# A gated linear attention with a feed-forward layer: pairs of chunks in an order made by a list scheduler

## The chip, the cores and the metric

The kernel runs on one core of one Trainium2 chip. The core has five engines that run side by side, each in its own order: TensorE (PE, matrix products), VectorE (DVE), ScalarE (ACT), GpSimd (POOL) and SyncE (SP, which issues most of the transfers). The metric is the device time of one execution in microseconds (us), the median of several runs.

## The reference

Per batch (4), head (8) and step (768) a complex gate of width 48 decays a state of 48 x 48; q reads it. Then each of the 3072 tokens of 384 goes through a normalised two-layer product.

```python
mag = np.sqrt(a_re * a_re + a_im * a_im)
scale = np.minimum(mag, 0.999) / (mag + 1e-06)
...
for t in range(S):
    new_re = ar * S_re - ai * S_im
    new_im = ar * S_im + ai * S_re
    S_re, S_im = (new_re + kv, new_im)      # kv = k[t] (x) v[t]
    y[:, :, t] = np.einsum('bhd,bhde->bhe', q[:, :, t], S_re)
...
xn = (x - mu) / np.sqrt(var + 1e-06) * g_ln
out = x + np.maximum(xn @ w_ch1, 0.0) @ w_ch2
```

## The kernel before

The steps are cut into 24 chunks of 128 (six per batch), number n. Four chunks make a group, number qi; a group has two blocks of 256 steps. In a block's tiles of the gate, partition p holds steps 2p and 2p+1.

The log stage works on a whole group (the first group on one block at a time). ScalarE takes the logarithm `w` of a_re and 1/a_re (`g_log`), VectorE the ratio `r` of imaginary to real part and its square `r2` (`g_ratio`), ScalarE log(1 + r2) (`g_log1p`), VectorE the log of the magnitude `l` (`g_decay`), ScalarE the angle `th` = arctan r (`g_angle`). ScalarE has one table of functions for logarithm and exponential and one for arctan and sine, and loads the one that is needed (`table`).

Sums over the steps are matrix products with triangular matrices. `s_decay` sums `l` for a block with `u_f`, in matmuls of 64 rows that lie in the two halves of the array by turns, and ScalarE makes the growth `en` and the decay `e` of it. `s_phase` sums the angle for one chunk, twice: the first for the sine, the second a quarter turn on for the cosine. Each sum has two matmuls of 64 rows with `u_th` (L406) and one with `pick` (L409), which adds the running phase that VectorE carries from chunk to chunk in `car` (L413). The low 16 bits of the sum are the fraction of a turn, and ScalarE takes the sine of both (`trig`). `s_total` and `s_total2` make the decay of a whole chunk (`et`, `dec`).

GpSimd scales k by `en` and q by `e` (`s_scale`, L421, tiles `ke` and `qe`); VectorE multiplies each by cosine and sine (`s_stack`, `ks` and `qs`). Per chunk, TensorE transposes both (`transp`), forms the scores (`amat`), the next state (`state`, tile `G`) and the output x (`yout`), and transposes x (`xtr`). VectorE and ScalarE carry the results from the sum memory. The feed-forward layer (MoE in the code) works on a group, 512 tokens: `mm1` with 512 columns, ScalarE's Relu, then `mm2` per chunk, VectorE's last step `ot`, and the store. The weights are scaled by `moe_g_ln` and centred once, by column means from TensorE (`w_scale`, `w_centre`).

SP issues the loads of the gate, of k and q, and the stores. GpSimd's queue issues four loads of v and the two weight loads, each of which also casts to 16 bits.

The order comes from `PLACES`, a table of numbers in units of chunks: each step is put at its chunk's number plus its place, and `plan.run()` emits the steps sorted by it. GpSimd keeps the order as written; for the other engines the framework may still order what is ready. The first group has an order written out by hand.

Of the kernel before, what the change touches and what calls it, by code (L numbers as in the profile page):

```python
# [24 lines left out]
class Plan:  # L25


    def __init__(self):
        self.items = []

    def add(self, at, thunk):
        self.items.append((at, len(self.items), thunk))

    def spread(self, lo, hi, thunks):
        for i, t in enumerate(thunks):
            self.add(lo + (hi - lo) * (i + 0.5) / len(thunks), t)

    def run(self):
        for _, _, t in sorted(self.items, key=lambda x: x[:2]):
            t()  # L40


class Ledger:


    def __init__(self):
        self.keys = set()

    def step(self, made, needs):
        for key in needs:  # L50
# [5 lines left out]
     'load_qk_step': 1.29,
     'table_log': -1.2,
     'log': -1.36,  # L60
     'ratio': -0.91,
     'log1p': -0.58,
     'decay': -0.03,
     'sum': 0.72,
     'sum_step': 0.02,
     'total': 0.75,
     'total2': 6.05,
     'table_trig': 1.15,
     'angle': 1.51,
     'phase': 2.17,  # L70
     'phase_step': 0.59,
     'ke': 1.89,
     'ke_step': 0.17,
     'qe': 1.75,
     'qe_step': 0.6,
     'stack_k': 3.93,
     'stack_q': 3.62,
     'stack_step': 1.02},
 2: {'load_a': -7.2,
     'load_qk': -0.53,  # L80
     'load_qk_step': 1.29,
     'table_log': -1.2,
     'log': -0.78,
     'ratio': -0.59,
     'log1p': -0.14,
     'decay': -0.03,
     'sum': 0.75,
     'sum_step': 0.02,
     'total': 0.73,
     'total2': 5.58,  # L90
     'table_trig': 1.04,
     'angle': -0.31,
     'phase': 1.21,
     'phase_step': 0.21,
     'ke': 1.89,
     'ke_step': 0.16,
     'qe': 1.16,
     'qe_step': 0.77,
     'stack_k': 3.93,
     'stack_q': 3.62,  # L100
     'stack_step': 1.02},
 3: {'load_a': -7.56,
     'load_qk': -0.59,
     'load_qk_step': 1.29,
     'table_log': -1.2,
     'log': -0.86,
     'ratio': -0.75,
     'log1p': -0.48,
     'decay': -0.03,
     'sum': 0.42,  # L110
     'sum_step': 0.14,
     'total': 0.7,
     'total2': 5.71,
     'table_trig': 1.31,
     'angle': 0.73,
     'phase': 1.31,
     'phase_step': 0.1,
     'ke': 1.02,
     'ke_step': 0.16,
     'qe': 2.24,  # L120
     'qe_step': 0.02,
     'stack_k': 3.88,
     'stack_q': 3.65,
     'stack_step': 0.07},
 'first': {'ks': -1.65, 'qs': -1.23, 'amat': 0.63, 'state': 0.9, 'yout': 1.0, 'xtr': 1.46},
 'chunk': {'ks': 0.42, 'qs': 0.18, 'amat': 1.14, 'state': 2.6, 'yout': 2.06, 'xtr': 2.49},
 'moe': {'mm1': 6.4, 'mm1_len': 1.89, 'mm2': 8.05, 'mm2_len': 1.88},
 'rstd': 7.32,
 'end_log': -2.06,
 'load_v': -5.9,  # L130
 'w_lo': 2.93,
 'w_hi': 6.07,
 'second': {'ks': -0.32, 'qs': -0.41, 'amat': 0.99, 'state': 1.69, 'yout': 2.49, 'xtr': 3.13},
 'start': -2.01,
 'start_step': 0.09}
# [3 lines left out]
def kernel(  # L139
# [29 lines left out]
    consts = ctx.enter_context(tc.tile_pool(name="consts", bufs=1))
    wts = ctx.enter_context(tc.tile_pool(name="wts", bufs=1))  # L170
    ld = ctx.enter_context(tc.tile_pool(name="ld", bufs=2))
    pr = ctx.enter_context(tc.tile_pool(name="pr", bufs=1))
    stk = ctx.enter_context(tc.tile_pool(name="stk", bufs=2))
    att = ctx.enter_context(tc.tile_pool(name="att", bufs=2))
    msb = ctx.enter_context(tc.tile_pool(name="msb", bufs=2))
    pa = ctx.enter_context(tc.tile_pool(name="pa", bufs=4, space=PSUM))
    pb = ctx.enter_context(tc.tile_pool(name="pb", bufs=2, space=PSUM))

    ctx.enter_context(tc.manual_schedule(engines={mybir.EngineType.Pool}))

    def bank(shape, dtype, name):
        return pa.tile(shape, dtype, tag="a", name=name)

    def two_banks(name):
        return pb.tile([C, 2, 512], FP32, tag="b", name=name)


    Q = [dict() for _ in range(NQ)]
    X = [dict() for _ in range(N)]
    V = {}  # L190
    step = Ledger().step

    def load_a(qi, k_):

        b, blk = divmod(qi * QB + k_, NCH // R)
        step(("a", qi, k_), [])
        for name, ap in (("are", a_re), ("aim", a_im)):
            if name not in Q[qi]:
                Q[qi][name] = ld.tile([C, QB, H, R * D], FP32, tag=name, name=name)
            nc.sync.dma_start(  # L200
                out=Q[qi][name][:, k_],
                in_=ap[b].rearrange("h (k p j) d -> p k h (j d)", p=C, j=R)[:, blk])

    def load_qk(qi, m):
        step(("qk", qi, m), [])
        b, c = divmod(qi * QC + m, NCH)
        for name, ap in (("k", k), ("q", q)):
            X[qi * QC + m][name] = ld.tile([C, H, D], FP32, tag=name, name=name, bufs=6)
            nc.sync.dma_start(out=X[qi * QC + m][name],
                              in_=ap[b].rearrange("h (c p) d -> p c h d", p=C)[:, c])  # L210

    def load_v(b):
        step(("v", b), [])
        V[b] = ld.tile([C, H, NCH, D], BF16, tag="v", name="v", bufs=3)
        nc.gpsimd.dma_start(out=V[b], in_=v[b].rearrange("h (c p) d -> p h c d", p=C))

    load_a(0, 0)
    load_a(0, 1)


    ident = consts.tile([C, C], BF16)
    make_identity(nc, ident)

    u_f = consts.tile([C, R, C], FP16)
    u_hi = consts.tile([C, R, C], FP16)
    for t, base in ((u_f, 0), (u_hi, C)):
        nc.gpsimd.memset(t, 1.0)
        nc.gpsimd.affine_select(out=t, in_=t, pattern=[[-1, R], [1, C]], compare_op=ALU.is_ge,
                                fill=0.0, base=base, channel_multiplier=-R)
    nc.gpsimd.affine_select(out=u_hi, in_=u_hi, pattern=[[0, R], [0, C]], compare_op=ALU.is_ge,  # L230
                            fill=0.0, base=-HALF, channel_multiplier=1)
    nc.vector.tensor_tensor(out=u_f, in0=u_f, in1=u_hi, op=ALU.add)
    u_th = consts.tile([C, R, C], FP16)
    nc.vector.tensor_scalar(out=u_th, in0=u_f, scalar1=INV2PI, scalar2=None, op0=ALU.mult)


# [419 lines left out]
```

## Time and profile before

| | us |
|---|---|
| runs | 268.26, 269.4, 336.7 |
| median | 269.4 |
| profiled execution, span from first to last instruction | 266.8 |
| profiled execution's own time | not listed apart; the two runs that lie together are 1.5 and 2.6 above its span |
| TensorE busy | 214.6 |
| ScalarE, VectorE, GpSimd busy | 172.0, 168.4, 65.6 |

Busy times are of the span of one execution. Engines overlap, so they don't add up to it; an engine is the limit only in a stretch in which it has no idle time, and for that one looks at windows of the span.

### The profile page before, as it was taken

To read this page: it belongs to the slowest core of one execution; us is meant where nothing else is said; L and a number is where in the kernel's file an instruction comes from. 1 tells how busy PE (TensorE), PEld (TensorE's weight loads), DVE (VectorE), ACT (ScalarE), POOL (GpSimd) and SP (SyncE) were. 2 spreads that over 40 slices of the span, in tenths; PEclk is the share of its full clock that TensorE was granted. 3 is DMA by queue.
4 is the path that set the end of the run, shared out by engine and by line. 5 is a ranking of instruction groups with operands and counts; after the bars stand their busy time and mean duration, and the time that the engine had idled before them with its cause. 6 is when DMAs were issued, how large, how long until landed. Compare 5 with 4: busy or idle time off the path is not lost.

```text
span 266.8 us, 4741 instructions
## 1 busy us (share of the span) xinstructions
PE 214.6 (80%) x1937; PEld 126.4 (47%) x1953; DVE 168.4 (63%) x280; ACT 172.0 (64%) x199; POOL 65.6 (25%) x90
## 2 busy tenths in 40 slices
PE   0136733248834999999999999999999999999994
PEld 0001313036421556564576555655557677656452
DVE  1434237767877889976699557986588466645011
ACT  4353571482999769996499785998858723751530
POOL 8390008452401940039100090000900000000000
PEclk9999999999985899999799999999999999999999
DMA  7999925999999995727990052000100011001102
GB/s 204 239 272 193 167 45 144 246 189 158 137 183 266 203 140 88 194 74 160 165 90 0 33 117 62 32 0 32 59 0 32 2 59 63 0 2 60 61 29 88
DMA packets 105350, 28.62 MB, mean 107 GB/s; under 512 B 100336, under 2 KB 104944, under 8 KB 105328
## 3 DMA queue, kind: packets, MB, share of 16 engines
q1 hardware_dynamic: 78736, 23.60, 40.6%
q0 software_dynamic: 26592, 4.72, 21.6%
q8 instruction: 15, 0.25, 0.4%
q14 instruction: 7, 0.06, 0.1%
HBM read 28.31 MB, written 4.72 MB: 124 GB/s over the span
## 4 chain that ended last, share of the span: by engine, by line
PE 58%; ACT 17%; DMA 10%; DVE 8%; POOL 3%; issue 2%; SPq 2%; POOLq 0%
PE o L534 17%; PE hps L524 11%; DMA k<-in_k_dram 10%; PE tps L406 7%; PE tp L440 5%; PE tps L409 4%; PE at L452 3%; DVE r L332 3%; ACT r L309 2%; ACT h L527 2%; ACT are L309 2%; ACT w L309 2%; PE lps L368 2%; PE gm L474 2%; ACT L305 2%
## 5 line engine op out<-in xcount | busy, mean ns | idle before, releaser
L534 PE MATMUL o<-w2b,h 128*128 128x384 bf16 x288 | 52.3, 333 | 0.0
L524 PE MATMUL hps<-xT,w1b 128*128 128x512 bf16 x202 | 50.3, 379 | 0.9 <-ACT h L527 0.2
L527 ACT ACTIVATE h<-hps 128x1024 bf16<-128x1024 f32 x36 | 36.5, 1021 | 11.4 <-PE hps L524 11.3
L309 ACT ACTIVATE trig<-tps 128x768 bf16<-128x768 int16 x24 | 19.5, 811 | 27.2 <-DVE car L413 25.6
L534 PEld LDWEIGHTS <-h 128*128 128x128 bf16 x288 | 27.6, 100 | 18.7 <-issue 3.5
L537 DVE SCALAR_TENSOR_TENSOR ot<-o,rstd,x 128x384 f32<-128x384 f32 x24 | 14.8, 617 | 31.5 <-PE o L534 31.5
L454 DVE TENSOR_TENSOR atm<-at,mask 128x1024 bf16<-128x1024 f32 x24 | 29.1, 1213 | 7.1 <-PE at L452 6.9
L387 POOL COPY et<-et 4x384 bf16<-4x384 bf16 x6 | 4.7, 788 | 113.7 <-ACT et L309 113.7
L406 PE MATMUL tps<-th,u_th 64*128 64x384 f16 x96 | 26.4, 358 | 7.6 <-ACT th L309 7.6
L524 PEld LDWEIGHTS <-w1b 128*128 128x128 bf16 x216 | 19.6, 98 | 18.9 <-issue 0.5
L443 ACT COPY qsT<-tp 96x1024 bf16<-96x1024 bf16 x24 | 24.1, 1005 | 4.1 <-PE tp L440 4.1
L368 PE MATMUL lps<-l,u_f 64*128 64x384 f16 x48 | 7.7, 420 | 20.8 <-DVE l L348 20.8
L421 POOL TENSOR_TENSOR ke<-k,en 128x384 bf16<-128x384 f32 x24 | 21.3, 906 | 11.2 <-DMA k<-in_k_dram 7.1
L421 POOL TENSOR_TENSOR qe<-q,e 128x384 bf16<-128x384 f32 x24 | 22.0, 933 | 1.6 <-ACT e L309 1.2
L413 DVE TENSOR_SCALAR car<-tps 32x384 f16<-32x384 int16 x20 | 11.3, 563 | 16.6 <-PE tps L409 16.3
L496 ACT CAST x<-y 128x384 bf16<-128x384 f32 x24 | 11.3, 472 | 16.1 <-PE y L493 16.0
L440 PE MATMUL tp<-ident,qs 128*96 128x128 bf16 x192 | 16.7, 232 | 4.1 <-DVE G L478 4.1
L305 ACT ACT_TABLE_LOAD x14 | 18.0, 1283 | 1.0 <-PEq L642 0.8
L332 DVE TENSOR_TENSOR r<-aim,are 128x1536 f16<-128x1536 f32 (+1 forms) x7 | 10.9, 1562 | 11.9 <-ACT are L309 11.9
L440 PE MATMUL tp<-ident,ks 128*96 128x128 bf16 x192 | 17.2, 233 | 1.3 <-DVE ks L428 1.3
L443 DVE COPY ksT<-tp 96x1024 bf16<-96x1024 bf16 x24 | 16.3, 678 | 2.8 <-PE tp L440 2.6
L409 PE MATMUL tps<-car,pick 128*128 128x384 f16 (+1 forms) x48 | 17.5, 365 | 0.2 <-DVE car L413 0.2
(72 smaller groups left out, 362.8 us busy)
## 6 DMA issues: line engine op xcount, KB each, us to landing
are<-in_a_re_dram SPq DMA_DIRECT2D x12, 384.0 KB, 4.7
aim<-in_a_im_dram SPq DMA_DIRECT2D x12, 384.0 KB, 4.9
k<-in_k_dram SPq DMA_DIRECT2D x24, 192.0 KB, 4.3
q<-in_q_dram SPq DMA_DIRECT2D x24, 192.0 KB, 4.1
out_dram<-ot SPq DMA_DIRECT2D x24, 192.0 KB, 1.8
v<-in_v_dram POOLq DMA_DIRECT2D x4, 576.0 KB, 15.3
w1b<-in_moe_w_ch_dram POOLq DMA_DIRECT2D x1, 1152.0 KB, 9.7
w2b<-in_moe_w_ch_dram POOLq DMA_DIRECT2D x1, 1152.0 KB, 17.7
```

Source lines behind the costliest of these rows:

```text
L305: chain(nc.scalar.preload_act_table_set({"log": "natural_log_exp_and_others", "trig": "trig_and_small"}[name]))
L309: chain(nc.scalar.activation(**kw))
L332: nc.vector.tensor_tensor(out=cut(r, bs), in0=cut(Q[qi]["aim"], bs), in1=cut(Q[qi]["are"], bs), op=ALU.mult)
L406: nc.tensor.matmul(heads(ps[:, s]), lhsT=u_th[ts(i, HALF), j], rhs=steps(Q[qi]["th"], k_, i, j), start=(j == 0), stop=False)
L409: nc.tensor.matmul(ps[:, s, 0:DM], lhsT=pick[rows, s], rhs=cars[n % 2][rows], start=False, stop=True)
L421: eng.tensor_tensor(out=t[:, m], in0=X[qi * QC + m][which].rearrange("p h d -> p (h d)"), in1=Q[qi]["en" if which == "k" else "e"][:, m], ...
L440: nc.tensor.transpose(ps[:, h], Q[qi][which][:, m, h].rearrange("p a d -> p (a d)"), ident)
L443: (nc.scalar.copy if which == "qs" else nc.vector.tensor_copy)(out=t, in_=ps)
L454: nc.vector.tensor_tensor(out=x["atm"], in0=ps, in1=mask.unsqueeze(1).to_broadcast([C, H, C]), op=ALU.mult)
L524: nc.tensor.matmul(ps[:, ji], lhsT=w1b[:, dc, ts(jp * 2 + ji, C)], rhs=Q[qi]["xT"][:, dc].rearrange("p c t -> p (c t)"), start=(dc == 0), ...
L527: nc.scalar.activation(out=h[jp], in_=ps, func=AF.Relu)
L534: nc.tensor.matmul(ps, lhsT=Q[qi]["h"][j // 2][:, j % 2, ts(m, C)], rhs=w2b[:, j], start=(j == 0), stop=(j == NJ - 1))
```

## The change

The kernel is written anew around pairs of chunks (12 pairs, three per batch), with these parts:

- **Order.** Every step is an `Op` in a `Graph`: its engine (or two to choose from), a cost in us, what it needs, which buffers of which ring it uses (`RINGS`) and which banks of the sum memory. `order` places the steps one after another on five engines by their earliest start, and among those that could start soon takes the one with the smallest key (`KEYS` plus the pair's number). All five engines then keep that order.
- **Log stage** per pair, in units of one, one and then two pairs. The square may run on GpSimd or VectorE.
- **Sums.** For a pair, partition p holds steps 2p and 2p+1, and both kinds of sums run over all 128 rows. The phase is summed once per chunk; the carry is made once per pair.
- **Cosine.** ScalarE takes the sine of the angle and of its half (`sh`); the cosine is 1 - 2 sh^2, on GpSimd or VectorE (`f_cos`).
- **Choices of engine.** Scalings of k and q on GpSimd or VectorE; copies of the transposes on VectorE or ScalarE.
- **MoE** on a pair, 256 tokens: matmuls of 256 columns.
- **Weights.** Scaling and centring are one matrix product of the weights with `gc`, 27 matmuls; the two loads stand behind the constants on GpSimd.
- **v** is loaded in 32 bits by SP and cast by GpSimd. `rstd` is a power on GpSimd in place of a logarithm and an exponential on ScalarE.

```diff
-PLACES = {1: {'load_a': -7.56,
-     'load_qk': -0.53,
...
+KEYS = {"ld_a": -10.982, "ld_qk": -2.438, "ld_v": -1.699, "vcast": 4.3, "t_log": -4.145, "ln":
...
+    def order(self, keys):
...
+                    if len(op.alts) > 1:
+                        other = [x for x in op.alts if x != e][0]
+                        if free[other] + op.alts[other][0] < t + op.alts[e][0] - 0.01:
+                            continue
+                    ests.append((t, op))
...
+                t0 = min(x[0] for x in ests) + SLACK[e]
+                t, op = min((x for x in ests if x[0] <= t0), key=lambda x: (x[1].key, x[0]))
...
+    UNITS = [[0], [1], [2, 3], [4, 5], [6, 7], [8, 9], [10, 11]]
...
+    for i in range(2):
+        g.add(("wl", i), "POOL", 1.4, "wl", i, lambda i=i: wl(i), tail=6.7)
...
+            def wp(jb=jb, ec=ec, o=o):
+                for dc in range(ND):
+                    nc.tensor.matmul(bank(o), lhsT=gc[:, dc, ts(ec, C)],
+                                     rhs=w1r[:, dc, ts(jb, 512)], start=(dc == 0),
+                                     stop=(dc == ND - 1))
...
+        add(("v", P), "POOL", .82, lambda: nc.gpsimd.tensor_scalar(
+            out=T("v", P), in0=T("vf", P), scalar1=1.0, scalar2=0.0, op0=ALU.mult, op1=ALU.add),
+            needs=[("vf", P, 0), ("vf", P, 1)], uses=[("vf", P), ("v", P)], key="vcast")
...
+        def f_dec():
+            ps = bank2(("dec", P))
+            for c in range(R):
+                for j in range(R):
+                    nc.tensor.matmul(heads(ps[:, c, 0:DM]), lhsT=u_e[:, c, j], rhs=step(T("l", P), j),
+                                     start=(j == 0), stop=(j == R - 1))
...
+        def f_ph():
+            ps = bank2(("ph", P))
+            rows = slice(0, 96) if first else slice(0, C)
+            for c in range(R):
+                nc.tensor.matmul(ps[:, c, 0:DM], lhsT=pick[rows], rhs=T("car", P)[rows],
+                                 start=True, stop=False)
+                for j in range(R):
+                    nc.tensor.matmul(heads(ps[:, c, 0:DM]), lhsT=u_th[:, c, j], rhs=step(T("th", P), j),
+                                     start=False, stop=(j == R - 1))
...
+        def f_cos():
+            eng = engine(("cos", P))
+            eng.tensor_tensor(out=T("sh", P), in0=T("sh", P), in1=T("sh", P), op=ALU.mult)
+            eng.tensor_scalar(out=T("trig", P)[:, 0], in0=T("sh", P), scalar1=-2.0, scalar2=1.0,
+                              op0=ALU.mult, op1=ALU.add)
...
+                def f_mm1(gi, part, o):
...
+                            nc.tensor.matmul(ps[:, jj], lhsT=w1b[:, dc, ts(gi * JG + jj, C)],
+                                             rhs=T("xT", P)[:, dc].rearrange("p c t -> p (c t)"),
+                                             start=(dc == 0), stop=(dc == ND - 1))
```

On GpSimd, before, from the scalings of the first group to the weight loads (`ke`, `qe` are scaled k and q, the number behind a name is that of its buffer):

```order
L421 TENSOR_TENSOR qe_222<-q_155,e_191 128x384
L215 DMA v_243<-in_v_dram 128x48x48
L387 COPY et_310<-et_310 4x8x48
L421 TENSOR_TENSOR ke_219<-k_157,en_189 128x384
L421 TENSOR_TENSOR ke_219<-k_161,en_189 128x384
L421 TENSOR_TENSOR qe_222<-q_159,e_191 128x384
L421 TENSOR_TENSOR qe_222<-q_163,e_191 128x384
L273 DMA w1b_146<-in_moe_w_ch1_dram 128x3x1536
L274 DMA w2b_147<-in_moe_w_ch2_dram 128x12x384
```

And now, from the last constants on (`v0<-vf0` is the cast of v for pair 0, `r21<-r1` the square for pair 1):

```order
L326 DMA w1r_178<-in_moe_w_ch1_dram 128x3x1536
L304 MEMSET sel_172 128x8
L307 MEMSET sel_172 64x1 x4
L308 MEMSET half_n_174 128x2
L328 DMA w2b_180<-in_moe_w_ch2_dram 128x12x384
L311 MEMSET cmat_175 128x1152
L313 AFFINE_SELECT cmat_175<-cmat_175 128x384 x3
L399 TENSOR_TENSOR qe0_110<-q0_70,e0_99 128x384
L390 TENSOR_SCALAR v0_78<-vf0_76 128x768
L399 TENSOR_TENSOR r21_88<-r1_85 128x768
L399 TENSOR_TENSOR ke1_109<-k1_74,en1_102 128x384
```

The weight loads stood behind the scalings of the first group and now stand ahead of the first of them; a cast of v and the square of pair 1 have come in, in this order.

On VectorE, before, in the middle of the program (`r` ratio, `r2` square, `l` log of the magnitude, `atm` masked scores, `ksT` copy of a transpose):

```order
L428 TENSOR_TENSOR ks_1643<-ke_1260,trig_1332 128x16x48
L332 TENSOR_TENSOR r_1576<-aim_383,are_381 128x1536
L454 TENSOR_TENSOR atm_1545<-at_1546,mask_131 128x1024
L498 BN_STATS stats_1539<-x_1537 128x6
L334 TENSOR_TENSOR r2_1577<-r_1576 128x1536
L499 BN_AGGR mv_1443<-stats_1539 128x2
L443 COPY ksT_1600<-tp_1591 96x1024
```

And now, at the ratios of pairs 6 and 7 (L399 is the helper of all products of two tiles, L360 that of the copies, L629 the last step `ot`):

```order
L399 TENSOR_TENSOR ks1_113<-ke0_108,trig1_104 128x16x48 x2
L399 TENSOR_TENSOR qs1_116<-qe0_110,trig1_104 128x16x48 x2
L629 SCALAR_TENSOR_TENSOR ot1_163<-banks_63,rstd2_154,x4_137 128x384
L360 COPY ksT0_118<-banks_63 96x1024
L360 COPY ksT1_119<-banks_63 96x1024
L399 TENSOR_TENSOR r0_84<-aim0_67,are0_64 128x768
L360 COPY qsT0_122<-banks_63 96x1024
L360 COPY qsT1_123<-banks_63 96x1024
L399 TENSOR_TENSOR ks2_114<-ke1_109,trig2_105 128x16x48
L399 TENSOR_TENSOR atm2_128<-banks_63,mask_171 128x1024
```

The square has left this stretch for GpSimd, the ratios are half as long, and copies of `qsT` stand beside those of `ksT`.

## Rows read from the trace of the kernel before

**Rows 1.** The page: busy us (share, instructions); DMA in tenths by 40 slices.

```profile
PE 214.6 (80%) x1937; PEld 126.4 (47%) x1953; DVE 168.4 (63%) x280; ACT 172.0 (64%) x199; POOL 65.6 (25%) x90
...
DMA  7999925999999995727990052000100011001102
```

**Rows 2.** Two windows: length, busy us of PE, PEld, DVE, ACT, POOL, clock, DMA, GB/s.

```profile
0.00:100.00 100.00, 53.44 (x415) 27.91 (x419) 59.78 (x88) 60.32 (x65) 41.01 (x62) 0.95 1.19 186
100.00:267.00 167.00, 161.17 (x1523) 98.44 (x1534) 108.62 (x193) 111.66 (x134) 24.62 (x28) 0.99 0.29 60
```

**Rows 3.** The chain that ended last, 40 to 75 us: start, us, what.

```profile
46.72 15.72 DMA k<-in_k_dram
...
62.50 9.83 DMA k<-in_k_dram
```

**Rows 4.** Timeline of SP's queue: start, us, what.

```profile
4.22 1.15 SPq L209 DMA_DIRECT2D k<-in_k_dram  x1
...
12.31 0.70 SPq L200 DMA_DIRECT2D are<-in_a_re_dram  x1
...
47.91 4.85 SPq L209 DMA_DIRECT2D q<-in_q_dram  x1
...
62.50 3.53 SPq L209 DMA_DIRECT2D k<-in_k_dram  x1
```

**Rows 5.** The page's DMA issues: size of each, us from issue to landing.

```profile
w2b<-in_moe_w_ch_dram POOLq DMA_DIRECT2D x1, 1152.0 KB, 17.7
```

**Rows 6.** Timeline of TensorE, phase sums.

```profile
121.99 0.50 PE L406 MATMUL tps<-th,u_th 64*128 64x384 f16 x2
...
122.69 0.49 PE L406 MATMUL tps<-th,u_th 64*128 64x384 f16 x2
```

**Rows 7.** The chain that ended last, TensorE at its full rate: start, us, what.

```profile
113.94 0.43 PE lps L368 x4
...
116.01 0.74 PE tot L381 x4
...
119.66 0.45 PE tp L440 x8
...
208.15 2.59 PE hps L524 x12
...
255.15 7.81 PE o L534 x48
```

**Rows 8.** Timeline of the first 40 us.

```profile
8.88 0.93 ACT L309 ACTIVATE r<-r,one_b 128x768 f16<-128x768 f16 x1 [2.93 <-POOL eps_b L264]
...
11.25 0.82 PE L368 MATMUL lps<-l,u_f 64*128 64x384 f16 x4 [11.25 <-DVE l L348]
...
17.44 0.80 PE L406 MATMUL tps<-th,u_th 64*128 64x384 f16 x2 [5.36 <-ACT th L309]
...
23.80 1.03 DVE L428 TENSOR_TENSOR ks<-ke,trig 128x768 bf16<-128x768 bf16 x2 [0.95 <-ACT trig L309]
```

**Rows 9.** Groups by line: count, busy us, mean ns, idle before.

```profile
L443 DVE COPY ksT<-tp 96x1024 bf16<-96x1024 bf16 x24 | 16.3, 678 | 2.8 <-PE tp L440 2.6
...
L421 POOL TENSOR_TENSOR qe<-q,e 128x384 bf16<-128x384 f32 x24 | 22.0, 933 | 1.6 <-ACT e L309 1.2 <-DMA q<-in_q_dram 0.4
...
L413 DVE TENSOR_SCALAR car<-tps 32x384 f16<-32x384 int16 x20 | 11.3, 563 | 16.6 <-PE tps L409 16.3 <-PE gm L474 0.2
```

**Rows 10.** Timeline, GpSimd and VectorE side by side.

```profile
42.46 1.77 POOL L421 TENSOR_TENSOR ke<-k,en 128x384 bf16<-128x384 f32 x2
...
43.48 3.31 DVE L334 TENSOR_TENSOR r<-r 128x1536 f16<-128x1536 f16 x1
...
44.20 1.77 POOL L421 TENSOR_TENSOR qe<-q,e 128x384 bf16<-128x384 f32 x2
...
108.35 0.95 DVE L334 TENSOR_TENSOR r<-r 128x1536 f16<-128x1536 f16 x1
```

**Rows 11.** A window of the first stage, columns as in Rows 2.

```profile
80.00:85.00 5.00, 1.75 (x8) 0.48 (x8) 4.13 (x7) 4.83 (x6) 0.00 (x0) 0.50 1.06 270
```

More of the change, by code (lines that the diff above doesn't have):

```diff
@@ L22 @@
 PSUM = bass.MemoryType.PSUM
[L25 to L52, printed above, removed]
@@ L56 @@
-PLACES = {1: {'load_a': -7.56,
-     'load_qk': -0.53,
[L58 to L135, printed above, removed]
@@ L155 @@
     NCH = S // C
-    N = B * NCH
     R = 2
-    QC = 4
-    QB = QC // R
-    NQ = N // QC
+    PB = NCH // R
+    NP = B * PB
     DM = H * D
@@ L166 @@
     HALF = C // R
+    JG = 4
+    NG = NJ // JG
     INV2PI = 1.0 / (2.0 * PI)
[L169 to L234, printed above, removed]
-    pick = consts.tile([C, 2, C], FP16)
-    nc.gpsimd.memset(pick, 0.0)
-    for s in range(2):
-        for row in (HALF + s, C - 1):
-            nc.gpsimd.affine_select(out=pick[:, s], in_=pick[:, s], pattern=[[0, C]],
+    UNITS = [[0], [1], [2, 3], [4, 5], [6, 7], [8, 9], [10, 11]]
@@ L242, with c_ue2, c_pick @@
+    def c_ue2():
+        nc.gpsimd.affine_select(out=u_e[:, 1], in_=u_e[:, 1], pattern=[[0, R], [0, C]],
+                                compare_op=ALU.is_ge, fill=0.0, base=-HALF, channel_multiplier=1)
+    def c_pick():
+        nc.gpsimd.memset(pick, 0.0)
+        for row in (HALF, C - 1):
+            nc.gpsimd.affine_select(out=pick, in_=pick, pattern=[[0, C]],
                                     compare_op=ALU.not_equal, fill=1.0, base=-row,
                                     channel_multiplier=1)
-    cars = []
@@ L556 @@
-    seq += [lambda m=m, w=w: s_scale(0, w, m) for w in "kq" for m in range(R)]
-    seq += [lambda w=w, a=a: s_stack(0, w, a, pair(0)) for w in "kq" for a in range(2)]
-    for i, t in enumerate(seq):
-        add(-30 + 0.1 * i, t)
-    seq = [lambda: load_v(0), lambda: g_angle(0, one(1)), lambda: s_phase(0, 2),
-            lambda: s_phase(0, 3), lambda: table("log"), lambda: g_log1p(0, one(1)),
-            lambda: g_decay(0, one(1)), lambda: s_decay(0, 1), lambda: s_total(0),
-            lambda: s_total2(0)]
@@ L598 @@
-    for g in range(NQ):
-        add(QC * g + P["rstd"], lambda g=g: rstd(g))
-    for i in range(2):
-        add(QC * (NQ - 1 + i) + P["end_log"], lambda: table("log"))
-    for b in range(1, B):
-        add(b * NCH + P["load_v"], lambda b=b: load_v(b))
-    for n in range(N):
-        o = P["first"] if n < R else P["second"] if n < QC else P["chunk"]
-        add(n + o["ks"], lambda n=n: transp(n, "ks"))
-        add(n + o["qs"], lambda n=n: transp(n, "qs"))
-        add(n + o["amat"], lambda n=n: amat(n))
-        add(n + o["state"], lambda n=n: state(n))
-        add(n + o["yout"], lambda n=n: yout(n))
-        add(n + o["xtr"], lambda n=n: xtr(n))
@@ L623, with c_ident, c_mask, c_sel @@
-    load_a(1, 0)
-    load_a(1, 1)
-    nc.sync.dma_start(out=gln, in_=moe_g_ln.rearrange("(dc p) -> p dc", p=C))
-    for m in range(QC):
-        add(P["start"] + 0.1 * m, lambda m=m: load_qk(1, m))
-    plan.run()
+        for t in tiles["car"]:
+            nc.gpsimd.memset(t, WINDOW)
+    def c_ident():
+        make_identity(nc, ident)
+    def c_mask():
+        make_upper_triangular(nc, mask, val=1.0, diag=True)
+    def c_sel():
+        nc.gpsimd.memset(sel, 0.0)
+        for k_ in range(R):
+            for i in range(R):
+                nc.gpsimd.memset(sel[ts(i, HALF), k_, ds(k_ * R + i, 1)], 1.0)
+        nc.gpsimd.memset(half_n, -0.5)
@@ L631 @@
+    for op in g.order(KEYS):
+        op.emit()
 _INS = ['q', 'k', 'v', 'a_re', 'a_im', 'moe_g_ln', 'moe_w_ch1', 'moe_w_ch2']
```

773 lines of the change are left out of this document (471 added, 302 removed), and 8 rows, old and new, of tables (KEYS, RINGS).

## The prediction

> **What bounds the kernel now.** I read the engines' busy times first. TensorE is busy 214.6 us of a span of 266.8, VectorE 168.4, ScalarE 172.0, GpSimd 65.6, and the DMA row is at 7 to 9 tenths for most of the first third, then nearly empty [rows 1]. Then two windows: from 0 to 100 us TensorE is busy 53.44 us, from 100 us to the end 161.17 of 167 [rows 2]. So there are two stages with two limits. In the second TensorE is full and only its own work counts. In the first it is half idle, and the chain that ended last says for what: it waits 15.72 and 9.83 us in a row for loads of k [rows 3]. The queue shows why. At the start SP passes eight loads of k and q in the 8.1 us between 4.22 and 12.31, about 1.0 us each; between 47.91 and 62.50 it passes three, 4.9 us each [rows 4]. That is while the two weight loads of GpSimd's queue run: the second lands 17.7 us after its issue [rows 5].
>
> **The change, part by part.** TensorE first, all at the rate of the second stage.
>
> Phase sums. Before, each of 24 chunks has two groups of two 64-row sums and one `pick`; one group takes 0.70 us from start to start (121.99 to 122.69) [rows 6]: 48 x 0.70 = 33.6 us. After, each of 12 pairs has two groups of three 128-row sums. A 128-row sum of the same strided 16-bit kind takes 0.74/4 = 0.185 (`tot`), a dense one 7.81/48 = 0.163 (`o`) [rows 7]. So a group costs 0.49 to 0.70; I take 0.56, from the nearest row, `tot`: 24 x 0.56 = 13.4. Gain 20.2 (16.8 to 21.8).
>
> Decay sums. Before, four 64-row sums take 0.43 together, since two halves of the array work side by side [rows 7]: 12 x 0.43 = 5.2. After, four 128-row sums follow one another: 12 x 0.74 = 8.9. Cost 3.7. The Trainium skill (TensorEngine Tiling, When to Use Tiling) says that a contraction of 64 rows is to be packed two to the array, which speaks against this part of the change. The trace agrees for the decay sums, 0.43 against 0.74; by that rule they would stay as they were and TensorE would have 3.7 us less to do.
>
> MoE. The first product goes from 512 to 256 tokens: 216 matmuls at 2.59/12 = 0.216 become 432. Eight matmuls of 128 columns, each with its own weights, take 0.45, 0.056 each [rows 7]; 256 columns lie between that and 0.163 for 384, at 0.109. 432 x 0.109 = 47.1 against 46.7: nothing. The second product is unchanged, 288 x 0.163 = 46.9.
>
> Weights. Nine column means become 27 products of 512 columns: +18 x 0.216 = 3.9. The total decays stay at 24 x 0.185 = 4.4; their spread to 96 rows goes from 48 to 56 small matmuls, +0.4.
>
> The rest per chunk (two transposes, scores, state, output, each eight heads or a little more) I price at 0.45 a piece: about 67 us with the transposes of x and the totals, the same before and after. TensorE in all after the change: 13.4 + 8.9 + 47.1 + 46.9 + 5.8 + 67 = 189 us; 12 less than before.
>
> ScalarE. Two evaluations per chunk as before (sine of the angle and of its half in place of sine and cosine), seven table loads and eleven copies fewer: below 172, and not the bound.
>
> VectorE. Twelve carries of 0.563 go (-6.8); eleven of the transposed copies of 0.678 come from ScalarE (+7.5) [rows 9]; 23 of the 48 scalings of k and q come from GpSimd, at about 0.55, an estimate below the 0.678 of a larger copy (+12.7). The other edits (squares to GpSimd, a smaller weight correction, two cosines, logs in halves) I put at -8, give or take 4. So 168.4 becomes some 174.
>
> GpSimd. It keeps 25 scalings of 0.93 (23 us) and takes ten squares, ten cosines of two steps and twelve casts of v, each on 768 columns. By the 384-column scaling that is 0.93 to 1.9 each; with 1.8 for two-input ones and 1.35 for the others, 18 + 31 + 16. About 88 us beside the constants, never full, but busy some 0.45 of the dense stage.
>
> Loads. v moves from four casting loads of GpSimd's queue to 24 plain ones behind SP: eight loads per pair, 8 us, against 189/12 = 15.8 us of TensorE for a pair. This hides, once the weights are through. But the weights now are issued behind the constants, at about 6 and 8 us instead of 46, beside the first inputs. For 17.7 us SP would pass four loads instead of seventeen: k and q of the first pair, and v of the first pair lands at about 27.5 instead of 15. What is queued behind it: on GpSimd the cast of v stands ahead of the square for pair 1, as the order shows, so pair 1's logs wait with it.
>
> **The first stage after.** In the kernel before, ScalarE's log of the first block starts at 8.88, after 2.93 of waiting for a constant, the sums start at 11.25, the phase sums at 17.44, and the products with sine and cosine at 23.80 [rows 8]. For pair 0 the steps stay: the constant comes first now, which takes off what it held up, a cosine is added, two of the four phase groups fall away; its products end near 24. Then v is last. Six loads of the two a's are out by 7 us, the next four (k, q) pass by 25, the two of v by 27.5. The cast ends at 28.9, the square at 30.7, and pair 1 repeats the steps of [rows 8]: log to sums 2.4, sums to phase sums 6.2, less two ScalarE operations like the 0.93 at 8.88 that stood between, plus some 2.7 for a total, two casts of x and the phase sums themselves: 40 us. On TensorE the weight products and all of MoE stand behind those phase sums, so the dense stage begins at about 40. Without the wait for v it would be 35, the square then standing behind pair 0's products. By then about 10 us of the 189 are done.
>
> **The dense stage.** 179 us remain for TensorE. VectorE has about 174 - 17 = 157 us in it. They are ordered by one list, each in its own order, so what one loses the other waits for. The loss that I see in the trace: VectorE's square at 43.48 took 3.31 us where its like takes 0.95; it stood still while GpSimd ran four scalings from 42.46 on and finished 0.8 us after them [rows 10]. So VectorE's operations on two SBUF inputs and GpSimd's exclude each other. Some 60 runs of such operations on VectorE (products, ratios, logs, scalings) meet GpSimd busy with a chance of 0.45; the wait is 0.55 for the rest of one operation and 2.4 for a row of four. That is 15 us at 0.55, 65 at 2.4, and none if the order keeps them apart. VectorE has 179 - 157 = 22 to spare, so I let half of the 15, 8 us, reach TensorE.
>
> **The sum.** 40 + 179 + 8, and 3.8 from the last `o` (255.15 + 7.81) to the end of the span, as now: 231. The profiled execution's span is 266.8, the median of the runs 269.4, so 2.6 lies around it: **233 us**, 0.865 of the median. A measurement here tells about 2% from no change.
>
> **Rivals.** *TensorE alone.* The order keeps the others out of its way, as in the second stage now, where it idles 6 of 167 us: 233 - 8 = 225, and 220 with the dense stage from 35. For: that stage now. Against: VectorE has less to spare.
>
> *The shared port sets the pace.* The mean wait is 1.3, half of the long one: 60 x 0.45 x 1.3 = 35, VectorE needs 157 + 35 = 192, and with the 8 us of mutual waiting 40 + 192 + 8 + 3.8 + 2.6 = 246; up to 260. For: [rows 10], and GpSimd's work doubled. Against: at 0.45 busy, rows of four are rare. The Trainium skill (SBUF — State Buffer, SBUF: two separate sides) calls this port pair an exclusive lock that one instruction holds to its end; the trace agrees, with 3.31 us for 0.95.
>
> *TensorE falls to the lower clock, and the kernel is slower.* Between 80 and 85 us, with TensorE busy 1.75 of 5, the granted clock is 0.50, which is 1.2 GHz [rows 11]; in the second stage it is 0.99. If waits for VectorE thin TensorE out, every us of its work takes two. From 40 + 179 x (1 + f) + 6.4 = 275 on it would be slower: f = 0.28, 50 us of dense work at the lower clock. Against: TensorE would have to be mostly idle over a quarter of the stage.
>
> **Chances.** The forecast (225 to 240) 0.42, TensorE alone (218 to 225) 0.20, the port (240 to 264) 0.25, the lower clock 0.06; 0.07 is left for a static order that meets late loads and ends within 2% of now. So faster 0.87, same 0.07, slower 0.06. The range of 219 to 255 takes in the first two cases and most of the third.
>
> **What would show it.** Right: TensorE nearly unbroken from about 40 us; a pair's phase sums in 1.1 us; the first load of v landing near 27 us; squares and products on VectorE stretched beside GpSimd. Wrong: a dense stage that starts before 33 or after 46; VectorE waiting for TensorE more than the reverse; 256-column matmuls well above 0.11; TensorE's clock below 0.95 after 45 us.

## The result, and the profile after

| | before | after |
|---|---|---|
| median of 4 runs, us | 268.83 | 248.11 |
| lowest and highest | 267.52, 336.7 | 247.52, 248.44 |
| span of the profiled execution | 266.8 | 246.7 |

The 336.7 is a disturbed execution; it is in the median before (268.26 without it), not in the ratio. The ratio is 0.921 (95% interval 0.915 to 0.927): faster, by 20.7 us from median to median, 20.2 without the disturbed execution. The prediction said 233 with a range of 219 to 255. The direction and the range held; the likeliest case (225 to 240) did not, and the time lies in the range of the rival in which the shared port sets the pace (246, 240 to 264).

The page of the kernel after, the lines that answer to [rows 1] and [rows 5]:

```profile
PE 198.2 (80%) x2123; PEld 147.2 (60%) x2123; DVE 192.3 (78%) x313; ACT 158.3 (64%) x193; POOL 104.0 (42%) x121
...
PEclk9999999799999999999999997999999999999999
DMA  7999898979984455928579044183421000001102
...
w2b<-in_moe_w_ch_dram POOLq DMA_DIRECT2D x1, 1152.0 KB, 17.9
```

TensorE is busy 16.4 us less, VectorE 23.9 more, GpSimd 38.4 more. Windows of the kernel after (length, busy us of PE, PEld, DVE, ACT, POOL, clock, DMA, GB/s), which answer to [rows 2]:

```profile
0.00:50.00 50.00, 19.74 (x147) 12.45 (x148) 20.72 (x38) 23.22 (x27) 18.02 (x39) 0.97 1.00 203
50.00:100.00 50.00, 45.13 (x484) 32.92 (x482) 48.29 (x73) 40.92 (x52) 28.60 (x27) 1.00 0.73 168
100.00:150.00 50.00, 44.24 (x508) 33.64 (x505) 48.29 (x77) 37.48 (x48) 27.98 (x25) 1.00 0.62 143
150.00:200.00 50.00, 46.36 (x513) 35.04 (x511) 45.91 (x76) 38.56 (x48) 21.23 (x21) 0.97 0.29 69
200.00:250.00 50.00, 42.77 (x481) 33.12 (x478) 29.14 (x52) 18.15 (x23) 8.13 (x10) 0.97 0.10 37
```

Two stages again, with other limits. The first 50 us are half idle. Then VectorE is busy 142.5 of 150 us, more than TensorE with 135.7; only in the last stretch does TensorE lead. The start of that kernel in its timeline (start, us, engine, line, what; in brackets what it waited for):

```profile
6.94 6.65 SPq L383 DMA_DIRECT2D k<-in_k_dram  x1
13.63 5.28 SPq L383 DMA_DIRECT2D q<-in_q_dram  x1
...
25.29 1.45 SPq L387 DMA_DIRECT2D vf<-in_v_dram  x2
25.39 0.56 DVE L399 TENSOR_TENSOR ke<-k,en 128x384 bf16<-128x384 f32 x1 [11.13 <-DMA k<-in_k_dram]
...
27.41 0.56 DVE L464 TENSOR_SCALAR car<-banks 32x384 f16<-32x384 int16 x1
28.01 0.81 ACT L470 ACTIVATE trig<-banks 128x768 bf16<-128x768 int16 x1 [9.30 <-DVE car L464]
...
28.85 0.56 DVE L399 TENSOR_TENSOR ks<-ke,trig 128x768 bf16<-128x768 bf16 x1 [0.88 <-ACT trig L470]
...
29.78 1.25 POOL L390 TENSOR_SCALAR v<-vf 128x768 bf16<-128x768 f32 x1 [1.14 <-DMA vf<-in_v_dram]
30.13 0.84 ACT L405 ACTIVATE w<-are 128x768 f32<-128x768 f32 x1
...
33.26 1.47 POOL L399 TENSOR_TENSOR r<-r 128x768 f16<-128x768 f16 x1 [2.23 <-DVE r L399]
...
46.19 0.85 PE L454 MATMUL banks<-th,u_th 128*128 128x384 f16 x2
```

Read it as one chain. The first load of k stands 6.65 us in SP's queue and is there only at 25.4, when VectorE has idled 11.13 us for it. The carry `car`, which needs only the phase sums, stands behind the scalings in VectorE's order, so it comes at 27.41; ScalarE's sine waited 9.30 us for it, and only then may ScalarE go back to logarithms, for pair 1, at 30.13. Pair 1's phase sums end at 47.

The groups of the dense stage (count, busy us, mean ns, idle before) show the second thing:

```profile
L399 DVE TENSOR_TENSOR qs<-qe,trig 128x768 bf16<-128x768 bf16 x24 | 21.7, 917 | 0.0
L399 DVE TENSOR_TENSOR ks<-ke,trig 128x768 bf16<-128x768 bf16 x24 | 19.3, 818 | 0.9 <-ACT trig L470 0.9
...
L360 DVE COPY ksT<-banks 96x1024 bf16<-96x1024 bf16 x19 | 12.4, 677 | 1.0 <-PE banks L507 1.0
...
L399 DVE TENSOR_TENSOR G<-banks,dec 96x384 bf16<-96x384 f32 x20 | 10.9, 545 | 2.4 <-PE banks L542 2.2
L423 DVE TENSOR_SCALAR l<-l 128x768 f16<-128x768 f16 x12 | 6.4, 535 | 0.4
```

The copy `ksT`, which reads the sum memory, takes 677 ns as in [rows 9]. The products `ks` and `qs`, which took 0.56 us each at the start, with nothing on GpSimd beside them (the row at 28.85), take 818 and 917 on average.

### The profile page after: what moved, and what is told of

It reads as the page before. It is cut to its first block, busy times and chain, and to the rows that moved or that the text cites. A ratio compares the mean times of both kernels' runs of the same rounds, so it can differ in the third digit from the quotient of the medians.

```text
span 246.7 us, 5275 instructions
## 1 busy us (share of the span) xinstructions
PE 198.2 (80%) x2123; PEld 147.2 (60%) x2123; DVE 192.3 (78%) x313; ACT 158.3 (64%) x193; POOL 104.0 (42%) x121
## 5 line engine op out<-in xcount | busy, mean ns | idle before, releaser
L623 PE MATMUL banks<-w2b,h 128*128 128x384 bf16 x288 | 55.6, 330 | 0.2 <-ACT h L614 0.2
L605 PE MATMUL banks<-xT,w1b 128*128 128x256 bf16 x432 | 53.2, 273 | 1.3 <-DVE xT L584 0.6
L605 PEld LDWEIGHTS <-w1b 128*128 128x128 bf16 x432 | 41.1, 98 | 8.7 <-DVE w1b L360 1.2
L614 ACT ACTIVATE h<-banks 128x1024 bf16<-128x1024 f32 x36 | 36.3, 1019 | 10.9 <-PE banks L605 10.8
L399 DVE TENSOR_TENSOR atm<-banks,mask 128x1024 bf16<-128x1024 f32 x24 | 28.6, 1214 | 3.1 <-PE banks L525 3.1
L399 POOL TENSOR_TENSOR r<-r 128x768 f16<-128x768 f16 x10 | 17.4, 1745 | 21.9 <-DVE r L399 21.9
L399 POOL TENSOR_TENSOR ke<-k,en 128x384 bf16<-128x384 f32 x13 | 14.1, 1101 | 27.2 <-ACT en L440 20.5
L629 DVE SCALAR_TENSOR_TENSOR ot<-banks,rstd,x 128x384 f32<-128x384 f32 x24 | 14.6, 609 | 10.5 <-PE banks L623 10.3
L476 POOL TENSOR_TENSOR sh<-sh 128x768 f16<-128x768 f16 x10 | 15.9, 1590 | 15.9 <-ACT sh L467 15.9
L399 DVE TENSOR_TENSOR qs<-qe,trig 128x768 bf16<-128x768 bf16 x24 | 21.7, 917 | 0.0
L399 POOL TENSOR_TENSOR qe<-q,e 128x384 bf16<-128x384 f32 x12 | 11.8, 988 | 20.3 <-DMA q<-in_q_dram 16.8
L399 DVE TENSOR_TENSOR ks<-ke,trig 128x768 bf16<-128x768 bf16 x24 | 19.3, 818 | 0.9 <-ACT trig L470 0.9
L435 PE MATMUL banks<-l,u_e 128*128 128x384 f16 x48 | 10.4, 342 | 11.7 <-DVE l L423 11.7
```

The costliest lines, as they stand in the source:

```text
L399: engine(name).tensor_tensor(**kw)
L435: nc.tensor.matmul(heads(ps[:, c, 0:DM]), lhsT=u_e[:, c, j], rhs=step(T("l", P), j), start=(j == 0), stop=(j == R - 1))
L476: eng.tensor_tensor(out=T("sh", P), in0=T("sh", P), in1=T("sh", P), op=ALU.mult)
L605: nc.tensor.matmul(ps[:, jj], lhsT=w1b[:, dc, ts(gi * JG + jj, C)], rhs=T("xT", P)[:, dc].rearrange("p c t -> p (c t)"), start=(dc == 0), ...
L614: add(("relu", P, gi), "ACT", .91, lambda gi=gi, o=o: act(out=T("h", P)[:, ts(gi, JG)], in_=bank2(o).rearrange("p s (j t) -> p (s j) t", t ...
L623: nc.tensor.matmul(bank(("o", n))[:, 0:DM], lhsT=T("h", P)[:, j, ts(c, C)], rhs=w2b[:, j], start=(j == 0), stop=(j == NJ - 1))
```

## The experiments

The first four, e9 and e12 keep the order of every engine as the changed kernel has it (e1, e9 and e12 but for the loads they move); in the others the scheduler orders anew. e2, e3, e4 and e12 leave out work, so their times are no goal for a whole kernel. The kernel before, run beside each, had medians of 268.0 to 269.9, so differences of a us between two runs are not read.

| run | us | to the kernel before, 95% interval |
|---|---|---|
| e1 weights late | 239.05 | 0.888 (0.881 to 0.895) |
| e2 GpSimd thin | 231.67 | 0.861 (0.855 to 0.867) |
| e3 TensorE thin | 240.54 | 0.894 (0.888 to 0.900) |
| e4 VectorE thin | 235.64 | 0.875 (0.869 to 0.881) |
| e5 squares on ScalarE | 233.02 | 0.870 (0.862 to 0.878) |
| e6 two pairs first | 244.26 | 0.912 (0.903 to 0.920) |
| e7 e5 and e6 together | 227.04 | 0.847 (0.841 to 0.853) |
| e8 GpSimd idle | 241.57 | 0.900 (0.893 to 0.907) |
| e9 keys first | 242.45 | 0.904 (0.899 to 0.909) |
| e10 two phase sums | 246.82 | 0.920 (0.914 to 0.925) |
| e11 order moved | 241.62 | 0.899 (0.894 to 0.904) |
| e12 e1 and e2 together | 225.61 | 0.837 (0.829 to 0.845) |

**e1.** The weights behind the first inputs.

```diff
-    for op in g.order(KEYS):
+    ops = g.order(KEYS)
+    late = [op for op in ops if op.name[0] == "wl"]
+    rest = [op for op in ops if op.name[0] != "wl"]
+    at = [op.name for op in rest].index(("qe", 0, 1)) + 1
...
+    for op in rest[:at] + late + rest[at:]:
         op.emit()
```

> The two weight transfers are issued on GpSimd's queue behind the second query scaling of pair 0 (about 28 us instead of 5 and 7), nothing else moves. Theory A (the first key load, slowed by the weights beside it, holds the start): k of pair 0 lands some 8 us earlier, the first rotated product ks goes from 28.9 to 20-22 us, the first Relu from 53.6 to about 46, and the time falls by 5 to 9 us, to 239-243. Rival (the chain of pair 1 or the later weights take its place): ks is early, but the first Relu stays at 51-55 and the time moves by less than 2 us.

Its timeline:

```profile
6.53 1.15 SPq L383 DMA_DIRECT2D k<-in_k_dram  x1
...
21.32 0.84 ACT L405 ACTIVATE w<-are 128x768 f32<-128x768 f32 x1
...
42.84 1.00 ACT L614 ACTIVATE h<-banks 128x1024 bf16<-128x1024 f32 x1
```

The load of k passes in 1.15 us, pair 1's logarithm starts 8.8 us earlier, the first Relu 10.7 earlier, and the time is 9.1 us less. VectorE's busy time stays at 192.2. All of this lies within theory A or goes further than it named: the late key held the start.

**e9.** The same end reached on the other queue: pair 0's loads ahead of the coefficients of pairs 1 and 2, the weights untouched.

```diff
...
+    first = [op for op in ops if op.name[:2] in (("k", 0), ("q", 0), ("vf", 0))]
+    rest = [op for op in ops if op not in first]
+    at = max([op.name for op in rest].index((nm, 0)) for nm in ("are", "aim")) + 1
+    for op in rest[:at] + first + rest[at:]:
```

> The changed kernel with one change on SyncE's queue alone: pair 0's key, query and value loads stand ahead of the coefficient loads of pairs 1 and 2; the weights go where they went. Theory A (the first stage waits for pair 0's key because 2.4 MB of coefficients and both weights are in flight before it): its first key scaling starts at 13-15 in place of 25.4, ks at 20-21, and the time falls by 4 to 9 us, to 239-244, as with late weights, as long as pair 1's coefficients land before 21. Rival (pair 1's coefficients, now behind, become last): its first logarithm goes from 30.1 to no earlier than 27, and the time moves by less than 3 us.

Its timeline:

```profile
14.20 0.55 DVE L399 TENSOR_TENSOR ke<-k,en 128x384 bf16<-128x384 f32 x1
...
25.92 0.84 ACT L405 ACTIVATE w<-are 128x768 f32<-128x768 f32 x1 [4.38 <-DMA are<-in_a_re_dram]
```

The time is as theory A has it (239 to 244), but its condition, pair 1's coefficients before 21 us, did not hold: the key comes 11.2 us earlier, then those coefficients are last, as in the rival, and pair 1's logarithm gains only 4.2; the time gains 5.7. So what counts at the start is the logarithm of pair 1, not the key as such.

**e2.** GpSimd's share of the scalings, squares, cosines and casts cut to 16 columns (one head dimension for v).

```diff
-                    (nm, P, c), out=T(nm, P)[:, c],
...
+                    n = 16 if g.ops[(nm, P, c)].eng == "POOL" else DM
+                    tt((nm, P, c), out=T(nm, P)[:, c, 0:n],
...
+        for nm in ("r2", "v", "trig", "ke", "qe"):
+            for t in tiles[nm]:
+                nc.gpsimd.memset(t, 0.5)
```

> Leaves out most of GpSimd's share of the scalings, squares, cosines and casts of v (16 of 384 or 768 columns, one head dimension of v); the order of all engines is that of the changed kernel. Theory A (VectorE sets the pace of the dense stage, and is stretched by GpSimd's SBUF traffic): ks and qs fall from 818 and 917 to about 550 ns each, VectorE's busy time from 192 to 171-175, and the time by 8 to 16 us, to 232-240. Rival B (VectorE's stretched operations would wait anyway, for TensorE or the chain): the operations shorten alike, but VectorE waits more and the time falls by less than 4.

Windows from 50 to 200 us, groups, and busy times on the page of this run:

```profile
50.00:100.00 50.00, 49.82 (x541) 36.76 (x540) 45.14 (x79) 44.83 (x57) 10.12 (x30) 0.98 0.75 170
100.00:150.00 50.00, 49.29 (x574) 38.30 (x572) 47.28 (x91) 41.85 (x53) 11.41 (x28) 1.00 0.64 148
150.00:200.00 50.00, 50.00 (x614) 40.89 (x613) 44.97 (x84) 40.51 (x50) 9.57 (x22) 1.00 0.21 53
```

```profile
L402 DVE TENSOR_TENSOR qs<-qe,trig 128x768 bf16<-128x768 bf16 x24 | 13.1, 561 | 0.0
L402 DVE TENSOR_TENSOR ks<-ke,trig 128x768 bf16<-128x768 bf16 x24 | 12.9, 550 | 1.0 <-ACT trig L476 0.9
L363 DVE COPY ksT<-banks 96x1024 bf16<-96x1024 bf16 x19 | 12.6, 680 | 2.1 <-PE banks L517 1.9 <-issue 0.2
```

```profile
PE 192.3 (84%) x2123; PEld 146.0 (64%) x2123; DVE 180.9 (79%) x313; ACT 156.9 (68%) x193; POOL 55.1 (24%) x134
```

`ks` and `qs` are back at 550 and 561, the copy from the sum memory has not moved, and TensorE is unbroken: 149.1 of 150 us. The time falls by 16.4 us, a little past theory A's 16; VectorE's 180.9 lies above the 171 to 175 expected, because of the first row below. GpSimd also delivers sooner here, which this run can't take apart from the wait. The clearing of the tiles, which the kernel after doesn't have, gave rows of its own:

```profile
9.63 12.04 DVE L429 TENSOR_SCALAR l<-l 128x768 f16<-128x768 f16 x1
...
9.66 1.42 POOL L313 MEMSET r<- 128x768 f16 x2 [1.69 <-DVE l L427]
11.01 2.77 POOL L313 MEMSET v<- 128x768 bf16 x4
...
20.41 1.05 POOL L314 MEMSET cmat<- 128x1152 f16 x1
...
33.05 0.84 ACT L408 ACTIVATE w<-are 128x768 f32<-128x768 f32 x1
```

An operation of 0.36 us took 12.04: it began beside a train of clears on GpSimd and ended with it (in e12, which clears on VectorE, the same operation took its 0.36 at the same place). That cost pair 1's logarithm 2.9 us (33.05 for 30.13), so the gain at an equal start is about 16.4 + 2.9 = 19.

**e3 and e4.** The same amount of work taken from TensorE and from VectorE: five of the twelve products of each second MoE matmul; and `ks` cut to one head.

```diff
-                    for j in range(part * JG, part * JG + JG):
+                    for j in {0: (0, 1), 1: (4, 5), 2: (8, 9, 11)}[part]:
```
```diff
-                    (nm, P, a), out=T(nm, P)[:, :, :, a],
...
+                    (nm, P, a), out=T(nm, P)[:, :, 0:H if nm == "qs" else 1, a],
...
```

> Leaves out 5 of the 12 products of each second MoE matmul, 19.5 us of TensorE's work, order unchanged. Theory A (VectorE is the bound from 50 to 220 us): the time falls only by what lies in the last 25 us, 3 to 7 us. Rival D (TensorE is the bound): the time falls by 15 to 20, to about 230.

> Cuts the products ks (24 of VectorE's operations, 19.6 us busy) to one head of 8, some 17 us less of VectorE's work, order unchanged; the output lacks those products. Theory A: the time falls by 8 to 14, to 234-240, after which TensorE is the bound. Rival D (TensorE is the bound): less than 4.

In both, pair 1's logarithm happened to start 1.2 to 1.3 us earlier (28.84 and 28.94 for 30.13). e3: 7.6 us less (3 to 7 expected), 6.3 at an equal start, for 19.5 us of TensorE's work. e4: 12.5 us less, 11.3 at an equal start, although VectorE's busy time fell by only 7.8 (192.3 to 184.5), as cut products still wait; 3.3 us of what is left is one wait on the clearing that this kernel needs, so the rest of VectorE lost 11. The timeline of e4:

```profile
71.30 0.22 DVE L402 TENSOR_TENSOR ks<-ke,trig 128x96 bf16<-128x96 bf16 x1
...
71.94 1.84 POOL L479 TENSOR_TENSOR sh<-sh 128x768 f16<-128x768 f16 x1
72.37 1.47 DVE L402 TENSOR_TENSOR ks<-ke,trig 128x96 bf16<-128x96 bf16 x1
```

The same product of 96 columns takes 0.22 us alone and 1.47 beside GpSimd's square, to whose end it runs (73.84 and 73.78). A us taken from VectorE counts fully, one from TensorE by a third: nearer to theory A than to D.

**e12.** e1 and e2 in one kernel; the tiles are cleared on VectorE.

> Late weights and the thin GpSimd together, order of the changed kernel held; leaves out what the thin kernel leaves out, and its tiles are cleared on VectorE in its idle time after 10 us instead of on GpSimd. If the start and the lock are two separate terms, their gains of 9.1 and 16.4 add: 221 to 225, which is the prediction's rival of TensorE alone (220 to 225). If one gain contains the other (VectorE, once free, would have made up for the late start): 228 to 231.

Its timeline, and its windows:

```profile
9.63 0.36 DVE L429 TENSOR_SCALAR l<-l 128x768 f16<-128x768 f16 x1
...
27.12 0.84 ACT L408 ACTIVATE w<-are 128x768 f32<-128x768 f32 x1
```

```profile
100.00:150.00 50.00, 49.85 (x600) 39.16 (x598) 46.63 (x85) 42.12 (x53) 10.01 (x25) 1.00 0.67 153
150.00:200.00 50.00, 50.00 (x615) 40.20 (x611) 45.80 (x85) 35.74 (x46) 9.10 (x20) 1.00 0.15 39
```

225.6, just above the 221 to 225 of two separate terms. The clears on VectorE delay the start here too: pair 1's logarithm is at 27.12, not at e1's 21.32. Against e2 it is 5.9 us earlier and the time 6.1 less. So in an order that is held the start counts about one to one, whether VectorE or TensorE is the limit behind it (e9, with 5.7 for 4.2, fits least well):

| kernel | logarithm of pair 1 starts | time |
|---|---|---|
| after | 30.13 | 248.1 |
| e9 | 25.92 | 242.5 |
| e1 | 21.32 | 239.1 |
| e2 | 33.05 | 231.7 |
| e12 | 27.12 | 225.6 |

**e11, e5 to e8, e10: orders made anew, all with the weights late.** First, what an order alone is worth.

```diff
-LATENCY = 0.16
+LATENCY = 0.2
```

> Late weights, and one constant of the scheduler (the delay between engines, 0.16 to 0.20) that changes no instruction but the order of many. If the work on the engines alone sets the time: within 1.5 us of 239. If the order counts as much as the moves tried so far: 3 to 8 us away, in either direction.

2.6 us more than e1: between the two expectations, and from this one sample the grain with which the next are read. It is not quite the same work, as the scheduler also chose anew between engines: five of GpSimd's operations went elsewhere (116 for 121).

```diff
-        add(("r2", P), "POOL", 1.7, lambda: tt(("r2", P), out=flat(T("r2", P)), in0=flat(T("r", P)),
-                                               in1=flat(T("r", P)), op=ALU.mult),
...
+        add(("r2", P), "ACT", .84, lambda: act(out=flat(T("r2", P)), in_=flat(T("r", P)),
+                                               func=AF.Square),
...
-            eng.tensor_tensor(out=T("sh", P), in0=T("sh", P), in1=T("sh", P), op=ALU.mult)
...
+        add(("sq", P), "ACT", .7, lambda: act(out=T("sh", P), in_=T("sh", P), func=AF.Square),
```

> Late weights as before, and the two squares of every pair (of r, and of the half-angle sine) go from GpSimd (and 2 of 12 from VectorE) to ScalarE, two activations of 0.8 us more per pair; the scheduler orders all engines anew. Theory A (operations of VectorE wait for GpSimd's to end, and VectorE sets the pace): GpSimd's busy time falls from 104 to 70-78, ks and qs to 650-750 ns, VectorE's busy time from 192 to 178-184, ScalarE's rises to 175, and the time falls from 239 to 229-235. Rival (ScalarE is the next bound, or the new order costs as much): 237 or more.

233.0, 6 us less than e1, as theory A has it: GpSimd 72.5 us busy, VectorE 175.5, `ks` and `qs` 654 and 575 ns (VectorE and `qs` fell further than the 178 to 184 us and 650 to 750 ns expected).

```diff
-    UNITS = [[0], [1], [2, 3], [4, 5], [6, 7], [8, 9], [10, 11]]
+    UNITS = [[0, 1], [2, 3], [4, 5], [6, 7], [8, 9], [10, 11]]
```

> Late weights, and the first activation-table unit holds pairs 0 and 1 together in place of one each, so that pair 1's logarithms no longer wait for pair 0's sines. Theory (after the weights are late, the chain of pair 1 through ScalarE's tables is what keeps TensorE at 6.6 to 7.1 of 10 us between 20 and 40 us): pair 1's first ks goes from 42.1 to about 30, pair 0's from 20.0 to 23-25, and the time falls by 3 to 8 us, to 231-236. Rival (the weights, or VectorE's total work, set the time anyway): within 2 us of 239.

> The changes of the two kernels ahead together. If the start and the dense stage are separate terms their gains add: 224-231. If both only bring VectorE's work nearer to one bound: no better than the better of the two by more than 2 us.

e6 missed both ways: pair 1's products come at 27.5 as meant, and the time is 5.2 us more than e1's. From 50 to 200 us no engine is full in it (TensorE 137.4 of 150, VectorE 127.3). With the squares on ScalarE the same units are 6.0 us better than the old ones (e7's 227.0 against e5's 233.0). e7 beats both kernels: 0.915 of the changed one's time. Why the units help there and hurt alone is not settled; 2.6 of it can be the order.

```diff
-                add((nm, P, c), "POOL", .9, lambda nm=nm, src=src, dc_=dc_, c=c: tt(
+                add((nm, P, c), "POOL" if (nm, P, c) == ("qe", 0, 1) else "DVE", .48, lambda nm=nm, src=src, dc_=dc_, c=c: tt(
...
-        add(("v", P), "POOL", .82, lambda: nc.gpsimd.tensor_scalar(
+        add(("v", P), "ACT", .74, lambda: nc.scalar.copy(out=T("v", P), in_=T("vf", P)),
```

> Late weights; GpSimd does no elementwise work on tiles of 384 or 768 columns after the first query scaling: key and query scalings and the cosine's last step on VectorE (25 more of 0.55 us and 11 of 0.36), squares and the cast of v on ScalarE (26 us more). Theory A (exclusive port): no operation of VectorE is stretched, ks and qs 550 ns, VectorE busy 181-187 in spite of 36 more operations, ScalarE 184, time 229-236. Rival B (GpSimd's help is worth more than its waits cost): VectorE busy above 190 and the time 239 or more.

Its page and groups:

```profile
PE 199.4 (83%) x2123; PEld 148.2 (62%) x2123; DVE 183.5 (77%) x346; ACT 180.5 (76%) x226; POOL 25.8 (11%) x55
```

```profile
L398 DVE TENSOR_TENSOR qs<-qe,trig 128x768 bf16<-128x768 bf16 x24 | 13.2, 549 | 0.0
```

The rows came as theory A said (549 ns, 183.5 us), the time did not: 241.6 instead of 229 to 236. With 12 us more on ScalarE and 8 on VectorE than e5, no engine is full from 50 to 150 us (TensorE 90.8 of 100, ScalarE 88.6, VectorE 86.2). Taking the waits away was not enough here. That the engines which got the work had too little to spare is likely but not shown; which chain holds this kernel stays open.

```diff
...
+                if name == "ph2":
+                    nc.tensor.matmul(ps[:, c, 0:DM], lhsT=pick[0:96], rhs=quarter[0:96],
+                                     start=False, stop=False)
...
-        add(("cos", P), "POOL", 2.5, f_cos, needs=[("sh", P)], uses=[("sh", P), ("trig", P)],
+        add(("cos", P), "ACT", .7, lambda: act(out=T("trig", P)[:, 0], in_=v16("ph2"), func=AF.Sin,
```

> Late weights, and the half-angle cosine is undone: a second phase sum per pair, a quarter turn on, on TensorE (8 products of 384 columns in place of none, about 15 us in all), whose sine ScalarE takes from PSUM; GpSimd loses the squares and the last step (25.5 us), VectorE two of each. Theory A (the lock costs more than TensorE's sums): VectorE's busy time falls from 192 to 176-182, TensorE's rises from 197 to 208-213, and the time is 233 to 240, no slower than with late weights alone (239). Rival D (TensorE's work sets the time, as the sum in the prediction took it): slower by 10 to 15, at 249-254.

TensorE 212.4 us busy (15.3 more than e1), VectorE 174.5 (17.7 less), and 246.8 us: 7.8 more than e1, between the two theories. So the half-angle cosine of the change is worth at most some 8 us, give or take an order's 2.6, half of what it saves TensorE. At most, because the second sum has four products here and had three in the kernel before: 24 of them at 0.163, some 4 us of TensorE, are this run's own. That the other half is paid on VectorE, which the squares cost 17.7 us, is a reading, not a test.

## Why the prediction was right or wrong

**TensorE's prices: right where they stand alone, 9 us short in all.** A phase group of three takes 0.48 us from start to start (0.56 taken, bounds 0.49 to 0.70), so 24 x 0.48 = 11.5 for 13.4. The first MoE product runs at 3.93/36 = 0.109 and the second at 7.81/48 = 0.163, as priced. In all TensorE was busy 198.2 us for the 189 of the sum. In e2 and e12, where it hardly stops, it is 192.3 and 192.1, so some 6 of the 9 come and go with GpSimd's work; the other 3 stay open. The timeline and the chain of the kernel after, which answer to [rows 6, 7]:

```profile
69.03 0.49 PE L454 MATMUL banks<-th,u_th 128*128 128x384 f16 x2
...
69.51 0.49 PE L454 MATMUL banks<-th,u_th 128*128 128x384 f16 x2
```

```profile
231.30 3.93 PE banks L605 x36
235.23 7.81 PE banks L623 x48
```

**The first stage: the step failed.** The prediction let pair 0's products "end near 24" and then named v as last, although the same paragraph had SP pass the loads of k and q only by 25: it carried the old times of [rows 8] over without asking whether the key was there. The products came at 28.85, and ScalarE's way back to logarithms, not GpSimd's cast, was the bottleneck; the square of pair 1 waited 2.23 us for VectorE's `r`, with `v` there at 29.8 (27.5 foreseen). Pair 1's phase sums ended at 47 for 40, the sign named as wrong ("after 46"): +7. Of these, 4 lie ahead of the end of pair 1's square (34.7 for 30.7) and 3 behind it, where the steps of [rows 8] took 12.3 us for 9.3. e1 and e9 show the cause from both queues. The Trainium skill (DMA: Bandwidth & Descriptors, Queues, rings and completion order) says that a DMA engine serves the queues that have work in turn; the trace fits that, with 6.65 us for a load of k beside the weights and 1.15 without them, but shows no single turn.

**The dense stage: right mechanism, too small.** VectorE's own work is 180.9 - 11.7 (the stalled row above) = 169 us in e2, for some 174. But its waits for GpSimd are 192.3 - 169 = 23 us, not 15, and in e2 they reach the end nearly whole, 19 us at an equal start, not half of 15. The assumption that failed is that VectorE has 22 us to spare that take up the rest: it was busy 95% from 50 to 200 us, and TensorE, which needs its products, follows it. GpSimd was also busier than priced, 0.52 of the time from 50 to 200 us for 0.45: the sum leaves out the two operations of `rstd` per pair, 13.3 us. The Trainium skill (SBUF — State Buffer, SBUF: two separate sides) has the port that the two engines share go to the one that comes first for its whole instruction; the trace agrees, with 1.47 us for 0.22 up to the end of GpSimd's square.

**The sum, mended.** Windows of the kernel after, split at 47 us, give the terms as they were. The start is 47 for 40 (+7). Behind it TensorE was busy 181.5 for 179 (+2.5; it had more to do than priced, but 16.7 rather than 10 were done by then). It stood idle 14.5 for 8 until the last `o` ended at 243.0 (+6.5), and 3.7 for 3.8 followed. Together that is the 246.7 of the span, for 231. In e2 TensorE is idle 0.9 over the same stretch (49.1 to 226.1 us there) in place of these 14.5, and busy 192.3 in all for 198.2: 19.5 us together, which is the 19 above. So GpSimd's work costs TensorE twice, in idle time and in longer busy time; the sum put the first at 8 and the second at nothing.

**The rivals.** The shared port's 246 came close by luck, by errors that cancel in the main: it took 35 us of waits (23) and a start at 40 (47). It also took half of 2.4 as 1.3; with 1.2 its waits are 32 and its time 243. TensorE alone (225, or 220 with the earlier start) is what e12, with little left on GpSimd, comes to: 225.6, or an estimated 220 with e1's start (5.8 us earlier); the prediction took too much of it for granted. TensorE's lower clock played no part: from 50 us on the granted clock is 0.97 to 1.00 in each window, with one of 32 slices at 0.7.

**Not settled:** e6 and e8, above. A kernel in which GpSimd keeps its times but not its traffic was not tried, so the part of e2's gain that comes from earlier deliveries isn't measured. Two things say that it is small: e4, which leaves GpSimd's work alone, gains 11.3 us for VectorE's 11; and in the kernel after, behind 47 us, no wait of VectorE or TensorE was ended by GpSimd, only four of ScalarE, 3.6 us together.
